# New lock rule and new due steps in the list scheduler of a recurrent-attention and gated-feed-forward kernel

## The chip, the cores and the metric

The kernel runs on one core of a Trainium2 chip. The metric is the time of one execution on the device in microseconds (us); less is better. The profile is of one execution.

## What is computed

There are 8 batches. Each has 8 heads of 512 tokens and 32 state vectors, all of width 64. In every head tokens attend to states and states attend to tokens:

```python
a     = softmax(scale * x @ state.T)      # 512 x 32
xread = a @ state                         # 512 x 64
a2    = softmax(scale * state @ x.T)      # 32 x 512
sread = a2 @ x                            # 32 x 64
attn  = concatenate([xread, sread])       # 544 rows
```

The heads are laid side by side (8 x 64 = 512 columns), which gives 4,352 rows: 8 batches of 512 token rows and 32 state rows. They go through a feed-forward block with 2,048 hidden columns:

```python
h = x @ w_in          # 512 -> 2048
g = h * cos(h)
y = g @ w_out         # 2048 -> 512
```

The result is float32. The two weight matrices arrive as float64, so the kernel fetches 64-bit words and converts them on the chip.

## The kernel before

**Tiles.** The work runs in the transposed sense: hidden columns on partitions, tokens along the free axis. For one batch a tile is 128 hidden columns by 512 tokens, so a batch has 16 tiles, and a pair of batches has 32. `hidden` (L488) makes a tile in a PSUM bank with two matmuls, because the kernel first multiplies the states into `w_in` (`products`, L312, with the copies out of PSUM at L462): the attention weights then meet that small product and `xread` is never formed. Then comes the gate, four instructions in turn: `gate` on ACT (L564, rounding to an integer), `gate2` on DVE (L567, the remainder), `gate3` on ACT (L570, the cosine as a shifted sine) and `gate4` on DVE (L584, the product with h, to `g_all`). A bank comes free with `gate4`; in the first pair tiles use two banks in turn.

**Product with w_out.** The first half of the first batch uses plain matmuls (`first_product`, `second_product`, L640). All later ones use a scheme with seven block products in place of eight: class `Product` (L772 matmuls), which needs sums and differences of the gated tiles (`sub`, L715, on POOL and DVE) and of the weight blocks (`sums_of`, L1325, and `inner_weight`, L689, on POOL). The weight blocks so made are sent to DRAM (`blocks_kept`, L677 and L692) and fetched back into a ring of four (L706). From the second pair on the hidden matmul has its own seven-product form (L543), for which POOL makes sums of the weights (`sw_sums`, L521). Tile 32 is the first of these.

**Weights.** Each 1 MB (or 0.5 MB) piece of the weights is fetched as 64-bit raw words (`fetch`, L210) and converted by five instructions (`convert`): two on ACT (L223, L226), two on DVE (L229, L232) and one on POOL (L237).

**Attention.** For each batch: scores (L312 to the banks `at0`, `at1`), row maxima (L325, L343), spreading of a value per row by a 32x32 transpose (L332), subtraction (L348), exponentials (L352, L361), sums (L325), the inverse (`inverse`, L373 and L374), normalising (`norm1`, L393). The late part turns the second softmax (L400, L405), reads (L417), scales (L427 or L436) and keeps (L441, L446) the new states.

**What sets the order.** From tile 32 on the order is written out: `plan`, `later_pair` and the tables by step. The first pair, tiles 0 to 31 with their attention, their weight conversions and weight sums, is ordered by a list scheduler that runs when the program is built. `first_pair_tasks` makes a list of tasks, each with an engine, an estimated cost, what it reads and writes, a due step, and a flag `shares` that says it uses the ports that DVE and POOL share. `link` turns data names into dependences and due steps into due times:

```python
t.due = 22.0 + PACE * t.due if t.due is not None else 1e9
for u in after[t]:
    t.due = min(t.due, u.due - t.cost - .1)
```

`first_pair` then repeats: for each engine it takes, of the tasks whose predecessors are done and that could start within `NEAR` (0.3) of the earliest, the one with the least due time plus a penalty for starting later; of the engines' candidates it issues the one that starts first. The order in which tasks are issued is the order of the instructions on each engine. Before the change the scheduler remembers one interval, the last POOL task's, and a DVE task with `shares` that would start inside it is moved to its end. POOL tasks are never moved.

Of the kernel before, what the change touches and what calls it, by code (L numbers as in the profile page):

```python
# [22 lines left out]
def kernel(  # L23
# [46 lines left out]
    TEMPS = 4  # L70
# [177 lines left out]
    class Attention:  # L248
# [207 lines left out]
        def products_kept(self, nt, bank=None, c0=0, c1=WC, copy=None,  # L456
                          js=(0, 1)):
            to = at if bank is None else side_banks
            if c0 == 0:
                sw_of[self.b, nt] = sw_all[:, nt % 2]  # L460
            for j in js:
                (copy or nc.scalar.copy)(sw_of[self.b, nt][:, j, c0:c1],  # L462
                                         to[j][:, c0:c1])
# [254 lines left out]
    class Product:  # L718
# [4 lines left out]
        def __init__(self, name, pr, row):  # L723
            self.name, self.pr, self.row = name, pr, (pr.n, row)
            self.n = len(products)
            self.b, self.c = acc[1 - self.n % 2], acc[self.n % 2]
            self.in_place = name in ("p3", "p7", "p4")
            self.frees = name in ("p3", "p6", "p7", "p4")
            products.append(self)
            self.first = len(stage_list)  # L730
            stage_list.extend((self, k) for k in range(len(ORDER)))
# [391 lines left out]
    def first_pair_tasks():  # L1123
# [49 lines left out]
        def attention(b, k):  # L1173
# [30 lines left out]
            m2 = k + 6 if b == 0 else k + 5  # L1204
            if b == 0:
                for j in range(2):
                    add("dve", .62, lambda j=j: a.sums1((j,)), f"z{z}{j}",
                        f"m1{j}", k + 5)
                add("dve", .46, a.inverse1, "m10 m11", "m10 m11", k + 5)
                for j in range(2):  # L1210
                    add("dve", .62, lambda j=j: a.spread1(slice(j, j + 1)),
                        f"m1{j}", f"xT{j}", k + 5)
                for j in range(2):
                    add("dve", .62, lambda j=j: a.norm1(slice(j, j + 1)),
                        f"z{z}{j} xT{j}", f"z{z}{j}", k + 5, True)
# [3 lines left out]
            if b == 0:  # L1219
# [4 lines left out]
                add("dve", .3, a.inverse2, "i20 i21", "i20 i21", m2 + 2)  # L1224
            else:
                add("act", 5.0, a.exps, "at0 at1 m20 m21",
                    f"z{z}0 z{z}1 xT2 xT3 i20 i21 m20 m21", m2)
                for j in range(2):
# [3 lines left out]
                    "m10 m11 i20 i21", k + 7)  # L1232
# [164 lines left out]
        def p5_tasks(k):  # L1397
# [3 lines left out]
            for i, (r, w) in enumerate(((lo, q1), (hi + " " + q1, q1),  # L1401
                                        (lo + " " + hi, q3)), 1):
                add("pool", 4 * pool(512), lambda i=i: pd.sums(i), r, w,
# [3 lines left out]
            for i in range(5):  # L1407
# [12 lines left out]
                elif i == 2:  # L1420
                    add("dve", .36, follow, "acc0 sums1", "sums2", at_)
                    add("pool", 4 * pool(512), lambda: pd.sums(4),
# [6 lines left out]
        def p3_sums(k):  # L1429
            pd = products_[1]  # L1430
            add("pool", 4 * pool(512), lambda: pd.sums(1),
# [17 lines left out]
        for step, what in (  # L1449
                (1, lambda: attention_late(0, 1)),  # L1450
                (3, lambda: products(0, 1, 3)),
                (3, lambda: add("pe", .4, lambda: states(1, side_banks[0]),
                                "held0", "sd00 sd01", 6)),
                (3, lambda: add("act", .53,
                                lambda: states_kept(1, side_banks[0]),
                                "sd00 sd01", "stT1", 6)),
                (5, lambda: attention(1, 5.0)),
                (7, lambda: products(0, 2, 7)),
                (11, lambda: products(0, 3, 11)),
                (13, lambda: products(1, 0, 15)),  # L1460
                (13, lambda: attention_late(1, 14)),
                (13, lambda: inner(0, a11, 5, temps[0], names(TEMPS), 15)),
                (15, lambda: sends(2, a22, 8, 17)),
                (15, lambda: sums_of(SQ, A21, A22, add_, 16, "pool")),
                (16, lambda: products(1, 1, 19)),
                (16, lambda: inner(3, matrix(SQ), SQ, temps[1], E, 15)),
                (17, lambda: sums_of(A22, SQ, A11, sub_, 18, "pool")),
                (17, lambda: attention(2, 18)),
                (18, lambda: sums_of(A21, A11, A21, sub_, 19, "dve")),
# [4 lines left out]
                (21, lambda: inner(4, matrix(A22), A22, temps[1], E, 21)),  # L1474
                (23, lambda: sums_of(SQ, A12, A22, sub_, 24, "dve")),
                (24, lambda: inner(6, matrix(SQ), SQ, temps[0], names(TEMPS),
                                   25)),
                (24, lambda: products(1, 3, 27)),
                (25, lambda: attention_late(2, 23.0)),
# [4 lines left out]
        for step, what in (  # L1484
                (26, lambda: outer(0, 2, 0, 0, 26, "dve")),
                (27, lambda: outer(0, 2, 0, 1, 27, "dve")),
                (28, lambda: tokens_of_next(30)),
                (28, lambda: products(2, 0, 28)),
                (28, lambda: p5_tasks(29.5)),
                (29, lambda: weight_columns(t32, 30)),  # L1490
                (29, lambda: add("dve", .7, lambda: halves(2, 0), "z00 z01",
                                 "E0", 30)),
                (29, lambda: add("dve", .7, lambda: halves(2, 1),
                                 "z00 z01 E0", "E1", 30)),
                (30, lambda: seven_tasks(t32, 30)),
# [4 lines left out]
        for step, t in enumerate(all_tiles[0:FIRST]):  # L1500
# [3 lines left out]
            if 4 <= step < 4 + NH:  # L1504
                first(step - 4, step + 1)
            for i in range(NH):
                if SECOND_AT[i] == step:
                    second(i, step + 2)
# [6 lines left out]
    CONV_DUE = (3, 4.5, 3.5, 6, 7.5, 7, 9, 9.5, 10.5, 11, 12, 14.5, 14, 15)  # L1515
    PACE, NEAR, SEND = 3.8, 0.3, 2.5

    def link(tasks):
# [20 lines left out]
        for t in reversed(tasks):  # L1539
            t.due = 22.0 + PACE * t.due if t.due is not None else 1e9  # L1540
            for u in after[t]:
                t.due = min(t.due, u.due - t.cost - .1)
# [11 lines left out]
    def first_pair():  # L1554
# [20 lines left out]
        pool_busy, cold = (0.0, 0.0), True  # L1575
        log = []
        while can:
            best = None
            for e in free:
# [4 lines left out]
                for t in mine:  # L1584
                    at_ = max(free[e], ready[t])
                    if t.shares and pool_busy[0] <= at_ < pool_busy[1]:
                        at_ = pool_busy[1]
                    starts[t] = at_
                soon = min(starts.values())
                t = min((t for t in mine if starts[t] <= soon + NEAR),  # L1590
                        key=lambda t: t.due + 1.0 * (starts[t] - soon))
                if best is None or starts[t] < best[0]:
                    best = starts[t], t
            at_, t = best
# [11 lines left out]
            if t.engine == "pool":  # L1606
                pool_busy = at_, end
# [139 lines left out]
```

## Time and profile before

| | |
|---|---|
| median of 3 runs | 739.78 us (738.67 to 739.96) |
| profiled execution | 740.65 us |
| its span, first to last instruction | 738.9 us |
| mean granted clock of TensorE | 0.993 |
| TensorE (PE) busy | 708.2 us, 96% |
| VectorE (DVE) busy | 506.8 us, 69% |
| ScalarE (ACT) busy | 347.3 us, 47% |
| GpSimd (POOL) busy | 542.5 us, 73% |
| first tile's matmul (L488) starts | 23.35 us |
| tile 31's last matmul (L488) ends, first pair over on TensorE | about 160.1 us |

The profiler gives one row for each instruction: its start, its length, its line in the kernel and, where its engine stood idle before it, what released it. A table of stretches gives the busy time of each engine between two moments. Rows on one engine may overlap by about 0.1 us, since the start of one instruction falls into the end of the one before. An instruction that waits inside the engine, for a port for example, shows as a longer row and not as idle time.

### The profile page before, as it was taken

What the parts mean: (1) busy time and instruction counts of PE and PEld (TensorE: products, weight loads), DVE (VectorE), ACT (ScalarE), POOL (GpSimd) and SP (SyncE); (2) the same over time, 40 slices, a digit from 0 to 9 for tenths busy, and PEclk for the clock granted to TensorE, in tenths of its full rate; (3) what the DMA queues carried; (4) which work ended last, traced back from release to release, by engine and by line L of the source; (5) the groups of instructions that cost most, each with busy time, mean ns of one, the idle gap of its engine ahead of it and who ended that gap; (6) DMA issues with size and microseconds to landing.
All of it is one profiled execution on the core that took longest, in us unless ns stands there. A gap on an engine that the chain in (4) does not pass through costs nothing.

```text
span 738.9 us, 10734 instructions
## 1 busy us (share of the span) xinstructions
PE 708.2 (96%) x3626; PEld 519.0 (70%) x3626; DVE 506.8 (69%) x703; ACT 347.3 (47%) x586; POOL 542.5 (73%) x524
## 2 busy tenths in 40 slices
PE   8898889999999999999999999999999999999997
PEld 3343343477778878777778788777688788888886
DVE  4989979957866668849756577768665467355550
ACT  5799675654463446343634464344634533211110
POOL 1557789375998997588998665879989665799600
PEclk9999999999999999999999999999999999999999
DMA  9966799536346964693238635762225466456662
GB/s 297 285 192 193 236 265 301 122 96 150 87 128 117 214 172 115 142 197 86 82 80 168 160 96 116 147 154 83 75 68 119 115 205 143 108 156 203 155 152 46
DMA packets 204021, 111.33 MB, mean 151 GB/s; under 512 B 149888, under 2 KB 166784, under 8 KB 203968
## 3 DMA queue, kind: packets, MB, share of 16 engines
q1 hardware_dynamic: 202880, 110.14, 57.4%
q8 instruction: 29, 0.48, 0.3%
q10 hardware_dynamic: 960, 0.39, 0.2%
q14 instruction: 24, 0.20, 0.1%
q0 software_dynamic: 128, 0.13, 0.1%
HBM read 87.03 MB, written 23.59 MB: 150 GB/s over the span
## 4 chain that ended last, share of the span: by engine, by line
PE 59%; POOL 21%; DVE 9%; issue 3%; DMA 3%; ACT 2%; SPq 1%; ACTq 0%; POOLq 0%; DVEq 0%
PE o L772 29%; POOL g_all L715 16%; PE h L543 13%; PE h L488 8%; POOL swS_all L521 3%; PE at L312 3%; PE at L877 2%; DMA held<-in_state_dram 2%; PE o L640 2%; POOL sw_all L521 2%; DVE g_all L715 1%; PE at L417 1%; DVE q_all L567 1%; DVE g_all L232 1%; DVE g_all L584 1%
## 5 line engine op out<-in xcount | busy, mean ns | idle before, releaser
L715 POOL TENSOR_TENSOR g_all<-g_all 128x512 f32<-128x512 f32 x252 | 332.5, 1349 | 61.8 <-DVE g_all L715 40.4
L772 PE MATMUL o<-g_all 128*128 128x256 f32 x1456 | 343.7, 381 | 2.4 <-POOL g_all L715 2.4
L772 PEld LDWEIGHTS o<-g_all 128*128 128x128 f32 x1456 | 273.7, 190 | 49.7 <-issue 5.7
L567 DVE TENSOR_TENSOR q_all<-q_all,h 128x1024 f32<-128x1024 int32 (+1 forms) x88 | 85.3, 971 | 40.7 <-ACT q_all L564 40.4
L564 ACT ACTIVATE q_all<-h 128x1024 int32<-128x1024 f32 (+1 forms) x88 | 73.1, 833 | 81.2 <-PE h L543 35.1
L584 DVE TENSOR_TENSOR g_all<-h,q_all 128x1024 f32<-128x1024 f32 (+1 forms) x88 | 85.7, 973 | 24.5 <-ACT q_all L570 23.6
L570 ACT ACTIVATE q_all<-q_all,halfpi 128x1024 f32<-128x1024 f32 (+1 forms) x88 | 84.2, 957 | 38.7 <-DVE q_all L567 38.5
L551 DVE TENSOR_TENSOR h<-h,sums_all 128x256 f32<-128x256 f32 x96 | 41.3, 430 | 77.5 <-PE h L543 60.2
L488 PE MATMUL h<-aT_all,sw_all 128*128 128x512 f32 x128 | 64.0, 628 | 13.0 <-DVE g_all L584 12.3
L543 PE MATMUL h<-aT_all,sw_all 128*128 128x256 f32 x192 | 59.6, 392 | 3.8 <-DVE g_all L584 3.4
L543 PE MATMUL h<-aS_all,swS_all 128*128 128x256 f32 x192 | 60.2, 395 | 2.6 <-ACT sums_all L529 1.8
L715 DVE TENSOR_TENSOR g_all<-g_all 128x1024 f32<-128x1024 f32 x42 | 62.0, 1490 | 0.1
L543 PE MATMUL h<-aS_all,sw_all 128*128 128x256 f32 x192 | 58.0, 384 | 0.1
L488 PEld LDWEIGHTS h<-aT_all,sw_all 128*128 128x128 f32 x128 | 23.2, 195 | 44.3 <-issue 21.5
L521 POOL TENSOR_TENSOR swS_all<-sw_all 128x128 f32<-128x128 f32 x48 | 22.5, 468 | 41.8 <-ACT sw_all L462 41.8
L543 PEld LDWEIGHTS h<-aS_all,swS_all 128*128 128x128 f32 x192 | 33.9, 189 | 27.0 <-issue 12.1
L780 ACT COPY o<-o 128x256 f32<-128x256 f32 x26 | 9.3, 357 | 85.1 <-PE o L772 85.1
L543 PEld LDWEIGHTS h<-aT_all,sw_all 128*128 128x128 f32 x192 | 34.5, 189 | 16.3 <-DVE g_all L584 12.2
L237 POOL TENSOR_TENSOR w_in<-w_in,aS_all 128x1024 int32<-128x1024 int32 (+1 forms) x10 | 22.3, 2241 | 29.9 <-DVE w_in L232 27.2
L787 ACT COPY o<-sums_all 128x256 f32<-128x256 f32 x26 | 9.8, 378 | 68.2 <-PE o L772 68.2
L543 PEld LDWEIGHTS h<-aS_all,sw_all 128*128 128x128 f32 x192 | 35.6, 190 | 8.2 <-DVE h L551 2.7
L607 DVE SCALAR_TENSOR_TENSOR held<-o,held 128x512 f32<-128x512 f32 x38 | 25.9, 681 | 13.7 <-PE o L772 13.1
(116 smaller groups left out, 931.6 us busy)
## 6 DMA issues: line engine op xcount, KB each, us to landing
g_all<-blocks_kept SPq DMA_DIRECT2D x206, 256.0 KB, 2.8
blocks_kept<-g_all SPq DMA_DIRECT2D x48, 256.0 KB, 3.9
g_all<-in_moe_w_out_dram SPq DMA_DIRECT2D x8, 1024.0 KB, 5.7
out_dram<-ot SPq DMA_DIRECT2D x128, 64.0 KB, 2.0
g_all<-in_moe_w_in_dram SPq DMA_DIRECT2D x6, 1024.0 KB, 7.1
x_b<-in_x_dram SPq DMA_DIRECT2D x24, 256.0 KB, 4.7
xT<-in_x_dram SPq DMA_DIRECT2D x80, 64.0 KB, 2.8
x_b<-in_x_dram SPq DMA_DIRECT2D x16, 128.0 KB, 4.3
```

The source lines that it names most:

```text
L237: nc.gpsimd.tensor_tensor(bits, bits, e, op=ALU.add)
L488: nc.tensor.matmul(out=t.hp, lhsT=t.lhs(i), rhs=t.rhs(i), start=(i == 0), stop=(i == t.kn - 1))
L521: nc.gpsimd.tensor_tensor(o, x1, x2, op=op)
L543: nc.tensor.matmul(out=out_, lhsT=w, rhs=r, start=start, stop=True, skip_group_check=True)
L551: nc.vector.tensor_tensor(o, h2[:, LO], sums_all[:, 0], op=ALU.add)
L564: nc.scalar.activation(t.q.bitcast(I32), t.hp, func=ACTF.Copy, bias=0.25)
L567: nc.vector.tensor_tensor(t.q, t.q.bitcast(I32), t.hp, op=ALU.subtract)
L570: nc.scalar.activation(t.q, t.q, func=ACTF.Sin, bias=halfpi, scale=-TWO_PI)
L584: nc.vector.tensor_tensor(g, t.hp, t.q, op=ALU.mult)
L607: nc.vector.scalar_tensor_tensor(out=out.t[:, ch], in0=bank, scalar=TWO_PI, in1=b.t[:, ch], op0=ALU.mult, op1=ALU.add)
L715: engine.tensor_tensor(o[:, i:i + n], x1[:, i:i + n], x2[:, i:i + n], op=ALU.subtract)
L772: nc.tensor.matmul(out=o, lhsT=ring[(self.first + k) % NB][:, i], rhs=g[:, i], start=(start and i == 0), stop=(i == QT - 1), skip_group_ch ...
```

## The change

The scheduler's model of the shared ports is replaced. There is now one time, `lock`, at which the ports come free. Every POOL task, and every DVE task with `shares`, starts no earlier than `lock`, and sets it to its own end. The penalty for starting later rises from 1.0 to 8.0 for each microsecond. Between engines that could start at the same time, the one whose task asked first goes first. Three kinds of DVE tasks get the flag: the inverses of the softmax sums and the differences of `halves`. The estimated cost of POOL's sums for the p5 and p3 products is halved (each makes two instructions of 512 elements a partition, not four). With this rule the due steps of nearly all tasks are set anew, `PACE` goes from 3.8 to 3.4, and the margin in `link` from 0.1 to 0.05. The test of when a batch's weight buffer is first written no longer asks for column 0, since the second half may now be copied first. No instruction of the computation changes.

```diff
-            if c0 == 0:
+            if (self.b, nt) not in sw_of:
                 sw_of[self.b, nt] = sw_all[:, nt % 2]
...
-            m2 = k + 6 if b == 0 else k + 5
+            m2 = k + 6 if b == 0 else k + 4
...
-                add("dve", .46, a.inverse1, "m10 m11", "m10 m11", k + 5)
+                add("dve", .46, a.inverse1, "m10 m11", "m10 m11", k + 5,
+                    True)
...
-                add("pool", 4 * pool(512), lambda i=i: pd.sums(i), r, w,
+                add("pool", 2 * pool(512), lambda i=i: pd.sums(i), r, w,
...
-                (1, lambda: attention_late(0, 1)),
-                (3, lambda: products(0, 1, 3)),
+                (1, lambda: attention_late(0, 0)),
+                (3, lambda: products(0, 1, 2.5)),
...
-                (5, lambda: attention(1, 5.0)),
-                (7, lambda: products(0, 2, 7)),
-                (11, lambda: products(0, 3, 11)),
-                (13, lambda: products(1, 0, 15)),
-                (13, lambda: attention_late(1, 14)),
+                (5, lambda: attention(1, 4)),
+                (7, lambda: products(0, 2, 4.5)),
+                (11, lambda: products(0, 3, 11.5)),
+                (13, lambda: products(1, 0, 16)),
+                (13, lambda: attention_late(1, 18)),
...
-                first(step - 4, step + 1)
+                first(step - 4, step - 1)
...
-                    second(i, step + 2)
+                    second(i, step)
...
-    CONV_DUE = (3, 4.5, 3.5, 6, 7.5, 7, 9, 9.5, 10.5, 11, 12, 14.5, 14, 15)
-    PACE, NEAR, SEND = 3.8, 0.3, 2.5
+    CONV_DUE = (3, 4.5, 3.5, 6, 6.7, 8.5, 9, 9.5, 12.0, 11, 11.3, 13.7, 12.5, 15.7)
+    PACE, NEAR, SEND = 3.4, 0.3, 2.5
...
-                t.due = min(t.due, u.due - t.cost - .1)
+                t.due = min(t.due, u.due - t.cost - 0.05)
...
-        pool_busy, cold = (0.0, 0.0), True
+        lock = 0.0
+        cold = True
...
-                    at_ = max(free[e], ready[t])
-                    if t.shares and pool_busy[0] <= at_ < pool_busy[1]:
-                        at_ = pool_busy[1]
-                    starts[t] = at_
+                    asked = max(free[e], ready[t])
+                    shares = t.shares or e == "pool"
+                    starts[t] = max(asked, lock) if shares else asked
                 soon = min(starts.values())
                 t = min((t for t in mine if starts[t] <= soon + NEAR),
-                        key=lambda t: t.due + 1.0 * (starts[t] - soon))
-                if best is None or starts[t] < best[0]:
-                    best = starts[t], t
-            at_, t = best
+                        key=lambda t: t.due + 8.0 * (starts[t] - soon))
+                asked = max(free[e], ready[t])
+                if best is None or (starts[t], asked) < best[0:2]:
+                    best = starts[t], asked, t
+            at_, _, t = best
...
-            if t.engine == "pool":
-                pool_busy = at_, end
+            if t.shares or t.engine == "pool":
+                lock = end
```

## The prediction

> **What bounds the kernel now.** I read the table of stretches first, then TensorE's waits, then the instructions in order of time, and last the order in which each kernel's instructions stand on their engines (no time is in that). The change touches only the first pair (tiles 0 to 31, until 160 us), so the question is what that part loses.
>
> ```profile
> 34.00:50.00 16.00, 15.07 (x77) 7.02 (x77) 12.01 (x20) 14.18 (x22) 9.55 (x5) 1.00 0.70 189
> 50.00:66.00 16.00, 16.00 (x66) 6.57 (x51) 15.22 (x21) 15.07 (x22) 12.16 (x7) 1.00 0.64 182
> 66.00:82.00 16.00, 11.67 (x60) 4.46 (x58) 15.73 (x20) 15.08 (x22) 11.11 (x6) 1.00 0.68 197
> 82.00:98.00 16.00, 11.30 (x61) 4.61 (x62) 15.77 (x16) 9.37 (x15) 12.67 (x7) 0.87 0.88 266
> 98.00:114.00 16.00, 15.58 (x60) 7.20 (x59) 12.30 (x14) 10.80 (x23) 15.84 (x10) 0.91 1.01 289
> 114.00:130.00 16.00, 14.84 (x67) 6.05 (x66) 15.93 (x22) 9.27 (x16) 15.84 (x12) 1.00 0.92 296
> 130.00:146.00 16.00, 15.66 (x68) 7.98 (x67) 14.52 (x20) 11.00 (x24) 6.61 (x5) 1.00 0.52 123
> ```
>
> The columns are PE, PEld, DVE, ACT and POOL busy, then TensorE's clock, DMA share and GB/s. Between 66 and 98 DVE is full (15.7 of 16) and PE is not (11.7, 11.3). That is the hole; from 98 on PE is nearly full, and from 250 to 700 it is 97 to 100% busy.
>
> ```profile
> PE h L488 <- DVE g_all L584: 12.3, 9, 3.5
> PE h L488 <- DVE aT_all L393: 0.7, 1, 0.7
> ```
>
> Of 14.4 us that PE idles in 20 to 162 us, 12.3 are nine waits of a tile's matmul (L488) for gate4 (L584) of the tile two before, which must give back the PSUM bank. So DVE's progress to L584 is the bound. What DVE loses is seen here:
>
> ```profile
> 83.19 3.40 DVE L232 SCALAR_TENSOR_TENSOR g_all<-g_all 128x1024 int32<-128x1024 int32 x1
> ...
> 83.17 2.34 POOL L237 TENSOR_TENSOR g_all<-g_all,aS_all 128x1024 int32<-128x1024 int32 x1
> ...
> 82.73 2.90 PE L488 MATMUL h<-aT_all,sw_all 128*128 128x512 f32 x4 [2.02 <-DVE g_all L584]
> ...
> 97.27 3.68 PE L488 MATMUL h<-aT_all,sw_all 128*128 128x512 f32 x4 [3.48 <-DVE g_all L584]
> ```
>
> L232 takes 1.22 us undisturbed; started with POOL's L237 it took 3.40, the 2.34 of POOL plus its own. Against the shortest row of each form, the stretched rows are: L232 +2.18 and +0.95; L229 +1.60, +0.46, +1.07, +1.07, +1.06; L373 +1.48; L393 +0.97; L1325 +0.48, +0.36. Sum 11.7 us in 50 to 103 us. L567 and L584, which read PSUM, stay at 0.68 throughout.
>
> **The change part by part.** No instruction of the first pair is added or removed except one 0.86 us warm-up matmul (11 become 12 after the opening two); everything else is order. After tile 31 the listed orders agree but for where one product stage stands among seven-product parts at the seam.
>
> *Opening.* ACT now puts the seventh conversion load (L223 to g_all), whose row waits for its transfer until 23.16, ahead of the copies of its weights (L462) out of PSUM, without which tile 0 cannot start. L223 1.05, L405 0.6, L462 twice 0.33: tile 0 can start at about 25.5, and with one read of 1.0 ahead of it at 25.9, not 23.35. Queued behind L223 are those copies and every gate; PE waits. But DVE does one L232 (1.13) after gate4 of tile 0 that it did before it, and gate4 waits only for its sine: ACT L564 at 27.7, L226, table load 1.28, L570 to 31.2, gate4 to 32.2, tile 2 at 32.6, not 34.21. Then the order turns on tile 3: L232, the inverse and four L427 (1.16) stand ahead of gate4 of tile 1, so tile 3 starts at 36.7 (was 36.05) and gate4 of tile 2 ends at 40.7 (was 40.63). Opening: 0, taken as a loss of 2.5 won back.
>
> *DVE from gate4 of tile 2 to gate4 of tile 14, the path to tile 16.* Counted start to start (L232, L715, L1325 1.13; L229, L567, L584 0.60; transposes and reductions 0.61), the order before has 42.4 us there, the new one 40.0: one weight sum (1.13), one L229 and one L567 (0.60 each) now stand later. It took 97.1 - 40.6 = 56.5 us, 14.1 more: 9.3 of the stretched rows above, 3.5 of idle (0.79, 1.54, 0.25, 0.54, 0.20, 0.19 in DVE's rows), 1.3 of small pieces. The new rule makes a ports task wait for the lock and, with weight 8 in place of 1, takes another task meanwhile; it also marks the inverses and the differences of `halves` as sharing, which L373 at 2.03 us says they are. Bounds: none of the 9.3 goes, or all.
>
> Row against rule: L232's 3.40 fits the Trainium skill, "SBUF — State Buffer", "Who interferes with whom": the pair is an exclusive lock and issue order, not the kind of operation, decides who blocks. That speaks against the change, since a list fixes order on one engine but not when POOL, freed by a semaphore, begins. By the rows avoided one by one the gain is 9.3; by the rule with drifting times it may be 0. I take half, 4.7, as the old scheduler had a lock test too and was still caught 11 times. Idle I put at 4.5, not 3.5: four times (tiles 7/8, 9/10, 10/11, 13/14) ACT now has the next tile's L564 ahead of this tile's sine. So 40.7 + 40.0 + 4.7 + 4.5 + 1.3 = 91.2 and tile 16 at 91.3, not 97.27: **6.0 us**.
>
> *PE from tile 16 to the end of tile 31.* One more first product (1.72) stands before tile 16, so 1.7 less is left, **+1.7**; it fits the hole, as PE idled there. Idle after tile 16 was 0.42 + 1.16 + 0.34 = 1.9; I allow 3.0, since DVE meets two L1325 and two L325 before gate4 of tile 22 and three L715 near tiles 24 to 26: **-1.1**.
>
> *Clock.* Tile 16 took 3.68 where 1.88 is usual, tile 13 2.90. By "TensorE: Matmul & The Clock Gate", "HAM oscillation — how this bites in real kernels", idle gaps over some 3.4 us slow the clock. The rows differ: the clock fell to 0.71 in 82 to 86 after gaps of 0.97 and 2.02 with PE busy 1.98 us of 78 to 82. By the rule the shorter gaps I expect cost nothing and tile 16's 1.80 comes back; by the rows it may stay. Half: **+0.9**.
>
> *POOL, SP.* POOL does one conversion and weight sums in another order; sends wait for the sums, nothing on PE waits for the sends in this stage. POOL idles 7.79 before L521 at 149.03 and again 4.79 and 5.00 at 165 to 177, so a backlog of several us is covered; without it, L521 (four of 0.46) is what seam parts of tile 32 would wait for. SP's opening five rows and its weight fetches keep their order; batch 2's x loads move by one send and batch 3's token loads behind the output stores, and their first reader (L294) is at 174, tens of us later. The scheduler's halved price of the p5 sums only alters places: 0.
>
> *After the seam.* The 580 us from tile 32 are the same queue, led by PE and by POOL in step; POOL's 5.00 wait at 176.75 ends with DVE's L715 of 175.49, itself in the fixed order. The block shifts as it is: 0.
>
> Sum 6.0 + 1.7 - 1.1 + 0.9 = 7.5 us. The profiled execution took 740.65 (span 738.9 and 1.75 around it), so 733.15; it stands 0.87 above the median 739.78, so the median should be 732.3. With none of the lock loss gone the sum is 2.8, with all of it 12.1: 737.0 to 727.7.
>
> **The rivals.**
>
> *The lock is the real bound and only moves.* Laid over each other, POOL's rows and DVE's sharing rows cover 74.4 of the 80 us from 50 to 130. If nothing of that work leaves the stretch, 5.6 us is all it can give, and stalls come back under other names: a gain of 2.8, 737.0. For it: POOL 15.84 of 16 twice. Against: the coverage holds waiting rows, and the sums can lag to 130 to 146, where POOL is busy 6.61 of 16.
>
> *Paired gates (slower).* At the four places named, tile n's bank comes free only after tile n+1's matmul, its conversion (0.5), sine (0.63) and gate4 (0.6) with latencies: about 2.5 us after PE ended tile n+1, of which PE has 1.0 to 1.7 of other work. I have counted about 1 us each. If a sharing instruction between them (L232 and two L393 stand at tiles 9 to 11) also meets POOL, each costs 1.2 more, and with a throttled restart of 1.8 each 4 us: 4 x 4 - 4 = 12 more than summed, so slower by 4.5, 744.3. It decides from about 2.9 us each on. For it: 2 us gaps throttled before. Against: DVE has the same number of such instructions as before.
>
> *POOL's backlog eats it at the seam.* If p5's first sums end past 148, not 134, tile 32's parts wait and the gain is swallowed: 0, 739.8. Against it the 7.79 us of POOL idle.
>
> *The change does nothing:* excluded, the order on every compute engine differs from about 20 us on.
>
> **How the numbers follow.** About 0.2%, 1.5 us, is what a measurement of this kernel can tell from no change. Summed forecast 0.62; lock only moves 0.18; paired gates 0.12; seam 0.08. Faster 0.62 + 0.18 = 0.80, same 0.08, slower 0.12. The range runs from all of the lock loss gone (728) to just short of no change (739), leaving out most of the slower case and of the seam case.
>
> **What would show it.** Right: last L488 of tile 31 ends near 152.6, not 160.07; tile 16 starts near 91; rows of L229, L232, L373 and L393 near their shortest; PE's wait for L584 falls from 12.3 to about 8; tile 0 starts near 25.9; the time from tile 32 to the end unchanged. Wrong: stretched DVE rows still add up to 10 us or more, L584 late at tiles 9 to 14 behind ACT L564, or L521 late at the seam.

## The result and the profile after

| | before | after |
|---|---|---|
| median of 5 runs each | 739.78 us (738.62 to 740.0) | 734.44 us (733.02 to 736.23) |
| profiled execution, its span | 740.65, 738.9 us | 736.23, 734.4 us |
| tile 16 starts | 97.27 us | 97.23 us |
| tile 31's last matmul ends (start of the instruction behind it) | 160.07 us | 155.54 us |

The changed kernel takes 0.993 of the time, 95% interval 0.991 to 0.9949: 5.3 us by the medians, 4.5 us between the two profiled spans. Predicted were 732.3 us and 7.5 us. The 4.5 us are all there when tile 31 ends; from there on the two traces run alike. The gain is not one of the clock: at a mean granted clock of 0.997 two runs of the changed kernel took 733.58 and 734.44 us, while eight runs of the kernel before, taken beside the experiments, took 738.37 to 740.84 us at 0.997 or 0.998.

The table of stretches of the changed kernel (PE, PEld, DVE, ACT, POOL busy, then TensorE's clock, DMA share, GB/s), in the same stretches as before:

```profile
34.00:50.00 16.00, 15.19 (x65) 7.03 (x64) 14.61 (x23) 15.62 (x24) 9.96 (x5) 1.00 0.67 180
50.00:66.00 16.00, 16.00 (x66) 6.62 (x65) 15.41 (x21) 14.03 (x22) 10.11 (x7) 1.00 0.60 197
66.00:82.00 16.00, 12.79 (x58) 4.76 (x56) 12.60 (x21) 12.72 (x17) 8.46 (x4) 0.89 0.60 193
82.00:98.00 16.00, 13.06 (x70) 6.01 (x71) 10.91 (x16) 14.36 (x27) 13.83 (x8) 1.00 0.74 226
98.00:114.00 16.00, 16.00 (x64) 7.51 (x63) 13.94 (x15) 9.39 (x16) 14.70 (x9) 1.00 0.87 239
114.00:130.00 16.00, 16.00 (x57) 6.65 (x55) 14.83 (x23) 11.61 (x20) 15.77 (x12) 1.00 1.00 318
130.00:146.00 16.00, 15.01 (x92) 6.84 (x92) 15.08 (x20) 10.87 (x25) 8.75 (x7) 1.00 0.76 175
```

Between 66 and 98 us DVE was full before; now it is busy 23.5 of 32 us, and PE still has a hole there (25.9 of 32). Neither engine is full: each waits for the other. The groups of DVE in 66 to 98 us of the changed kernel say what it waits for (busy, mean ns, then idle time ahead of the group and what ended it):

```profile
L584 DVE TENSOR_TENSOR g_all<-h,q_all 128x512 f32<-128x512 f32 x9 | 6.1, 690 | 4.1 <-ACT q_all L570 3.9
L232 DVE SCALAR_TENSOR_TENSOR g_all<-g_all 128x1024 int32<-128x1024 int32 x5 | 6.0, 1218 | 0.0
L567 DVE TENSOR_TENSOR q_all<-q_all,h 128x512 f32<-128x512 int32 x9 | 5.9, 675 | 4.0 <-ACT q_all L564 4.0
```

All five L232 of this group now take their undisturbed 1.22 us; before, five took 8.4 us in this stretch, 1.67 each. POOL's rows did not grow in exchange: it was busy 101.5 us of 18 to 160 before and 101.0 after. Instead DVE stands idle 8.1 us ahead of gate2 and gate4, for the rounding and the sine on ACT; before it was 0.4 us in that stretch. PE's waits in 20 to 162 us (total, times, longest):

```profile
PE h L488 <- DVE g_all L584: 5.6, 6, 1.9
PE at L417 <- ACT xT L405: 4.3, 3, 2.8
PE at L441 <- DVE sr L427: 0.6, 1, 0.6
```

The wait for gate4 fell from 12.3 to 5.6 us. And the instructions of PE in order of time, at the two places that matter below:

```profile
69.57 2.70 PE L488 MATMUL h<-aT_all,sw_all 128*128 128x512 f32 x4 [1.92 <-DVE g_all L584]
72.06 2.91 PE L640 MATMUL o<-g_all 128*128 128x512 f32 x4
...
93.69 1.98 PE L488 MATMUL h<-aT_all,sw_all 128*128 128x512 f32 x4 [1.07 <-DVE g_all L584]
95.51 1.88 PE L640 MATMUL o<-g_all 128*128 128x512 f32 x4
97.23 1.88 PE L488 MATMUL h<-aT_all,sw_all 128*128 128x512 f32 x4
```

Tile 9 waits 1.92 us and then it and the product behind it take 2.70 and 2.91 us instead of 1.88: the granted clock fell, to a mean of 0.59 in 70 to 74 us. Tile 16 starts as late as before, though it no longer waits; what is gained comes after it.

**How much DVE is stretched.** One number is used below for every kernel: over the rows of L229, L232, L373, L393, L507, L715 and the weight sums (L1325, here L1328) on DVE between 18 and 160 us, the busy time less the count times the undisturbed length (L232, L715 and sums 1.22 us for 1024 elements, L229 and L393 0.69 and 0.68, L373 0.17, half forms by their own shortest row). It is 20.8 us before and 13.7 us after. It is not by itself a measure of speed: in the table below e5_rule has the lowest value and is the slowest kernel, and e10_half has 17.2 and starts tile 16 first.

### The profile page after: what moved, and what is told of

It reads as the page before. It is cut to its first block, busy times and chain, and to the rows that moved or that the text cites. A ratio compares the mean times of both kernels' runs of the same rounds, so it can differ in the third digit from the quotient of the medians.

```text
span 734.4 us, 10738 instructions
## 1 busy us (share of the span) xinstructions
PE 707.4 (96%) x3628; PEld 518.9 (71%) x3628; DVE 499.6 (68%) x703; ACT 346.3 (47%) x586; POOL 541.2 (74%) x524
## 4 chain that ended last, share of the span: by engine, by line
PE 62%; POOL 21%; DVE 6%; ACT 5%; issue 3%; DMA 2%; SPq 1%; POOLq 0%; DVEq 0%; ACTq 0%
PE o L773 29%; POOL g_all L715 16%; PE h L543 13%; PE h L488 9%; POOL swS_all L521 3%; PE at L312 3%; PE o L640 2%; PE at L878 2%; DMA g_all<-in_moe_w_out_dram 2%; DVE g_all L715 2%; POOL sw_all L521 2%; PE at L417 2%; DVE g_all L584 1%; PE o L878 1%; DVE q_all L567 1%
## 5 line engine op out<-in xcount | busy, mean ns | idle before, releaser
L715 POOL TENSOR_TENSOR g_all<-g_all 128x512 f32<-128x512 f32 x252 | 333.5, 1354 | 59.5 <-DVE g_all L715 43.2
L543 PE MATMUL h<-aT_all,sw_all 128*128 128x256 f32 x192 | 59.6, 392 | 3.8 <-DVE g_all L584 3.4
L543 PE MATMUL h<-aS_all,swS_all 128*128 128x256 f32 x192 | 60.2, 395 | 2.6 <-ACT sums_all L529 1.8
L715 DVE TENSOR_TENSOR g_all<-g_all 128x1024 f32<-128x1024 f32 x42 | 60.9, 1465 | 0.1
L543 PE MATMUL h<-aS_all,sw_all 128*128 128x256 f32 x192 | 58.0, 384 | 0.2
L543 PEld LDWEIGHTS h<-aS_all,swS_all 128*128 128x128 f32 x192 | 33.9, 189 | 27.0 <-issue 12.1
L543 PEld LDWEIGHTS h<-aT_all,sw_all 128*128 128x128 f32 x192 | 34.5, 189 | 16.3 <-DVE g_all L584 12.1
L237 POOL TENSOR_TENSOR w_in<-w_in,aS_all 128x1024 int32<-128x1024 int32 (+1 forms) x10 | 21.4, 2153 | 29.9 <-DVE w_in L232 22.7
L543 PEld LDWEIGHTS h<-aS_all,sw_all 128*128 128x128 f32 x192 | 35.6, 190 | 8.3 <-DVE h L551 2.8
L607 DVE SCALAR_TENSOR_TENSOR held<-o,held 128x512 f32<-128x512 f32 x38 | 25.8, 680 | 13.7 <-PE o L773 13.1
```

The lines of the kernel that those rows point to most:

```text
L543: nc.tensor.matmul(out=out_, lhsT=w, rhs=r, start=start, stop=True, skip_group_check=True)
L607: nc.vector.scalar_tensor_tensor(out=out.t[:, ch], in0=bank, scalar=TWO_PI, in1=b.t[:, ch], op0=ALU.mult, op1=ALU.add)
L715: engine.tensor_tensor(o[:, i:i + n], x1[:, i:i + n], x2[:, i:i + n], op=ALU.subtract)
```

## The experiments

The variants of the changed kernel collect what the scheduler lists and move entries of that list before they are issued (`move` behind, `put` directly behind another entry), all dependences kept. Times are medians with lowest and highest; the ratio is to the kernel before, run on the same chip. Tile times are those of the profiled execution.

| kernel | median us | ratio, 95% interval | tile 9 | tile 16 | tile 31 ends | DVE stretched |
|---|---|---|---|---|---|---|
| before | 739.4 to 740.6 | 1 | 62.04 | 97.27 | 160.07 | 20.8 |
| after | 734.44 (733.02 to 736.23) | 0.993 [0.991, 0.9949] | 69.57 | 97.23 | 155.54 | 13.7 |
| e5_rule | 749.08 (743.89 to 753.07) | 1.0116 [1.0078, 1.0154] | 64.70 | 98.70 | 160.06 | 11.9 |
| e6_dues | 743.52 (742.74 to 746.05) | 1.0058 [1.0044, 1.0072] | 72.55 | 100.2 | 162.3 | 20.8 |
| e11_seam | 740.70 (739.25 to 741.96) | 1.0019 [1.0009, 1.0029] | 63.43 | 99.01 | 159.08 | 14.2 |
| e1_open | 735.33 (732.42 to 739.32) | 0.9943 [0.9921, 0.9966] | 67.28 | 96.63 | 155.6 | |
| e2_warm | 735.86 (732.25 to 736.78) | 0.9932 [0.9912, 0.9951] | 67.71 | 97.08 | 156.0 | |
| e3_gates | 736.16 (735.27 to 739.2) | 0.9954 [0.9937, 0.997] | 69.75 | 99.82 | 158.5 | |
| e4_both | 734.36 (733.91 to 735.4) | 0.9922 [0.9909, 0.9935] | 67.78 | 95.77 | 154.5 | 16.5 |
| e7_fill | 738.26 (736.86 to 738.75) | 0.9979 [0.9969, 0.9988] | 70.07 | 98.71 | 157.5 | |
| e8_best | 736.65 (736.37 to 737.46) | 0.9961 [0.9949, 0.9973] | 66.37 | 97.16 | 155.8 | 14.8 |
| e9_nofill | 735.92 (733.64 to 736.53) | 0.9953 [0.994, 0.9965] | 66.21 | 96.61 | 155.3 | 15.8 |
| e10_half | 734.11 (733.68 to 734.5) | 0.9934 [0.9921, 0.9948] | 66.15 | 94.19 | 152.95 | 17.2 |
| e12_early | 735.55 (735.37 to 737.81) | 0.9931 [0.9916, 0.9946] | 68.62 | 97.35 | 156.9 | |

**Which half of the change carries it: the rule or the due steps?**

e5_rule, the kernel before with the new rule:

```diff
-                    if t.shares and pool_busy[0] <= at_ < pool_busy[1]:
-                        at_ = pool_busy[1]
+                    starts[t] = max(asked, lock) if shares else asked
...
-                        key=lambda t: t.due + 1.0 * (starts[t] - soon))
+                        key=lambda t: t.due + 8.0 * (starts[t] - soon))
```

> The kernel before with the new rule of the shared ports alone (one release time, weight 8, the flags and the halved Pool costs); the due steps stay the old ones. Theory 1 (the rule carries the gain, by the DVE rows that a Pool operation no longer stretches): the stretched DVE rows between 18 and 160 us sum to about 14 us as in the changed kernel, not 21; tile 31 ends at 155 to 157 us instead of 160.1, and the time is 734.5 to 737. Theory 2 (the due steps carry it, by the order of conversions that they set, and the rule alone does little or harm): stretched rows may fall, but tile 31 ends at 159 or later and the time is 739 or more.

e6_dues, the changed kernel with the lock, the weight of 8 and the rule for ties turned back, and everything else kept:

```diff
-                    starts[t] = max(asked, lock) if shares else asked
+                    if t.shares and pool_busy[0] <= at_ < pool_busy[1]:
+                        at_ = pool_busy[1]
...
-                        key=lambda t: t.due + 8.0 * (starts[t] - soon))
+                        key=lambda t: t.due + 1.0 * (starts[t] - soon))
...
```

> The changed kernel with the old rule of the ports and the old weight of 1; the new due steps, flags and costs stay. Theory 1 (the rule carries the gain): stretched DVE rows return to about 20 us, tile 31 ends at 159 to 161 us, 738.5 to 741. Theory 2 (the due steps carry it): tile 31 ends at 155 to 157 us, 734 to 736.5, with stretched rows still near 20 us.

Neither theory was right: each half alone is slower than before, by 1.2% and 0.6%, and only both together are faster. With the due steps in place the rule is worth 1.3%, or 9 us (743.52 against 734.44). Its effect on DVE is confirmed: it takes the stretched rows from 20.8 to 11.9 us by itself, and the due steps alone leave them at 20.8. The same group of DVE, in 18 to 160 us, first of e6_dues, then of e5_rule:

```profile
L232 DVE SCALAR_TENSOR_TENSOR g_all<-g_all 128x1024 int32<-128x1024 int32 x8 | 13.2, 1655 | 0.2
```

```profile
L232 DVE SCALAR_TENSOR_TENSOR g_all<-g_all 128x1024 int32<-128x1024 int32 x8 | 9.7, 1222 | 0.1
```

How much of the 9 us is the shorter rows and how much the order that the new weight also changes was not separated. e6_dues loses its time ahead of tile 16 (2.9 us later than before): PE waits 2.22 us for POOL's conversion L237 and 2.07 us for gate4 there, and tile 9 and the product behind it then take 3.78 and 2.50 us.

In e5_rule tile 31 ends at 160.06 us, as before, and then the kernel loses 8.6 us more. The same instruction of the seam, the late product L312 into `at`, starts at 167.50 us before, at 162.98 after and at 176.06 in e5_rule. PE of e5_rule in order of time:

```profile
163.51 0.59 PE L543 MATMUL h<-aT_all,sw_all 128*128 128x256 f32 x2
163.94 0.59 PE L543 MATMUL h<-aS_all,swS_all 128*128 128x256 f32 x2
165.39 0.70 PE L543 MATMUL h<-aS_all,swS_all 128*128 128x256 f32 x2 [0.85 <-ACT sums_all L529]
165.93 0.59 PE L543 MATMUL h<-aT_all,sw_all 128*128 128x256 f32 x2
168.31 1.22 PE L543 MATMUL h<-aS_all,sw_all 128*128 128x256 f32 x2 [1.79 <-DVE h L551]
169.33 1.06 PE L543 MATMUL h<-aT_all,swS_all 128*128 128x256 f32 x2
```

The new rule listed the parts of the first seven-product tile one behind the other, after tile 31, where before and after have them spread between tiles and products. So each part waits for the sums of the last, and the clock falls too (0.79 in 162 to 178 us; from 168.31 on a row takes 1.06 to 1.22 where 0.59 to 0.70 is usual). The waits in these rows and the next are 3.2 us, the longer rows about 3, and four pairs of L543 more than before stand behind tile 31, 1.7 us. The six runs of e5_rule took from 743.89 us at a mean clock of 0.998 to 753.07 us at 0.984, so about half of the loss goes with the clock, and the rest is there without it.

e11_seam tests that: e5_rule with the new pace and, of the new due steps, only those from step 24 on.

```diff
-                (24, lambda: products(1, 3, 27)),
-                (25, lambda: attention_late(2, 23.0)),
+                (24, lambda: products(1, 3, 31)),
+                (25, lambda: attention_late(2, 25)),
...
-                (30, lambda: seven_tasks(t32, 30)),
+                (30, lambda: seven_tasks(t32, 29.5)),
...
-    PACE, NEAR, SEND = 3.8, 0.3, 2.5
+    PACE, NEAR, SEND = 3.4, 0.3, 2.5
```

> e5_rule (the kernel before with the new rule alone) with the new pace and those new due steps that stand at step 24 and later: the last products, the late part of the third attention, the sums of the second pair, and the first seven-product tile. Theory 1 (the rule alone lost its 9 us where that tile begins: its parts came behind tile 31, with waits and a clock of 0.79 at 162 to 178 us, and the late due steps put them between tiles 30 and 31 again): the waits of L543 between 163 and 173 us are gone and the time is 738 to 741, and what is left to the changed kernel (4 to 6 us) belongs to the early due steps. Theory 2 (the loss comes with the rule from the order of the early first products and gates): still 745 or more.

Theory 1 held: 1.0116 became 1.0019, the L312 of the seam is at 166.51 us, and no L543 waits there. So of the change's parts, the rule clears DVE, the late due steps together with the new pace repair the seam that the rule spoils, and the early due steps, with those of the conversions and the smaller margin, bring the rest: from 1.0019 to 0.993, some 6.6 us. Pace and late due steps were not tried apart. In e11_seam the cleared DVE is of no use, since PE then waits elsewhere, 8.3 us for gate4 and 4.4 for copies of weights out of PSUM (L462).

**Why the opening gave no lead.**

In the trace after, the opening is as predicted up to tile 0, but then slow. ACT, then PE, in order of time:

```profile
23.25 1.15 ACT L223 ACTIVATE g_all<-g_all 128x1024 f32<-128x1024 f32 x1 [2.23 <-DMA g_all<-in_moe_w_out_dram]
```

```profile
24.92 1.09 PE L417 MATMUL at<-x_b,xT 128*64 128x128 f32 x16 [2.78 <-ACT xT L405]
25.95 5.40 PE L488 MATMUL h<-aT_all,sw_all 128*128 128x512 f32 x8
```

Tiles 0 and 1 together take 5.40 us, where before they took 3.67. e1_open moves the conversion out of the way, e2_warm leaves it and puts three warm-up matmuls into the wait.

```diff
+        move(("convert", 6, "1"), ("turn_kept", 0, 1))
```

> The order of the changed kernel (734.4 us), one task moved: ACT's first conversion step of the seventh weight piece (L223 to g_all, whose transfer lands at about 23.2 us) goes behind the four copies that tile 0 and the first reads need. Theory: that step at the head of ACT's queue made TensorE wait 2.8 us, which delayed tile 0 from 23.35 to 25.95 and let its clock fall, so that tiles 0 and 1 took 5.4 us and not 3.7. Then tile 0 starts near 23.3, tiles 0 and 1 take 3.7, tile 2 starts 2 to 4 us before 34.7, and the time falls by 2 to 4 us, to 730.5 to 732.5. Rival: from tile 4 on ACT (15.6 of 16 us busy in 34 to 50) and DVE set the pace, so the head start is lost by tile 9 and the time stays at 734.4 within 0.7.

```diff
+        listed.insert(at_of(("reads", 0, 0)),
+                      (None, lambda: warm(3, acc[0]), None))
```

> The changed kernel with three more warm-up matmuls (2.6 us) on TensorE just before the first reads, in the 2.8 us for which it waits for ACT there. ACT's order stays. Theory: the clock fell because of that wait, so tiles 0 and 1 take 3.7 us instead of 5.4 while tile 0 still starts near 25.9; tile 2 starts up to 1.7 us earlier and the time falls by 1 to 1.7 us, to about 733. Rival: tile 2 waits for gate4 of tile 0 (ACT's table load and sine behind it) in any case and later engines set the pace: 734.4 within 0.7.

Both held the clock at the place: tiles 0 and 1 take 3.70 us in each. PE of e2_warm:

```profile
25.52 3.70 PE L488 MATMUL h<-aT_all,sw_all 128*128 128x512 f32 x8
```

Tile 2 then starts at 32.59 us in e2_warm and 32.02 in e1_open, not 34.71. (In e1_open tile 0 starts only 1.0 us earlier and PE still waits 2.19 us; L405 waited for DVE's norm1, until 23.29 us, instead of L223.) Yet tile 16 is at 97.08 and 96.63 us, and the ratios are those of the changed kernel within their intervals. Of a lead of 2.7 us in e1_open, 0.6 is left at tile 16. Tile 9 and its product are slow in both kernels, and 2.3 us of the lead are still there when tile 15 starts, 91.40 against 93.69 us. It goes here:

```profile
91.40 3.48 PE L488 MATMUL h<-aT_all,sw_all 128*128 128x512 f32 x4 [1.06 <-DVE g_all L584]
94.67 2.13 PE L640 MATMUL o<-g_all 128*128 128x512 f32 x4
```

In the changed kernel the same two took 1.98 and 1.88 us: 1.7 us of the lead are a fall of the clock. e2_warm loses 1.7 of its last 1.85 us at the same place.

**Are the paired gates the brake?**

e3_gates takes the gates of tiles 7/8, 9/10, 10/11 and 13/14 apart: on ACT gate of the second goes behind gate3 of the first, and on DVE gate2 of the second behind gate4 of the first. e4_both does this and e1_open's move.

```diff
+        for n in (7, 9, 10, 13):
+            move(("gate", n + 1), ("gate3", n))
+            move(("gate2", n + 1), ("gate4", n))
...
```

> The order of the changed kernel, with the paired gates of tiles 7/8, 9/10, 10/11 and 13/14 taken apart: gate of the later tile goes behind the sine of the earlier one on ACT, and gate2, gate3 and gate4 of the later one behind gate4 of the earlier one. Nothing else moves. Theory: the pairs made tiles 9, 11, 12 and 15 wait for a bank by 1.9, 1.0, 1.0 and 1.1 us, and the first of these waits also let TensorE's clock fall (1.9 us more at tile 9 and the product behind it). Then PE's wait for L584 falls from 5.6 to about 2 and the time falls by 2 to 5 us, to 729.5 to 732.5. Rival: the waits come from DVE's and ACT's whole load before tile 16, so they only change places: 734.4 within 0.7, or later by up to 1 us since gate4 of the later tile of each pair comes later.

> The opening as in e1_open and the gates as in e3_gates, together. If the two causes are apart the gains add: 4 to 8 us below 734.4, and tile 16 starts near 91, where the prediction had it. If the stretch to tile 16 is bound by DVE's and ACT's load, the sum is no better than the better of the two.

e3_gates gained nothing: 0.9954 against 0.993, the intervals overlap, and PE's wait for gate4 was 6.9 us. Its one run at a clock of 1.000 took 736.18 us, where that of the changed kernel took 733.02. e4_both is the lowest ratio of the study, 0.9922, but within the interval of the changed kernel; its clock was 0.998 or 1.000 in all five runs, and the fastest took 733.91 us, so its lead may be no more than the clock. So the pairs are not shown to cost anything by themselves.

**Does the clock take the leads?**

e7_fill puts zero-adding matmuls into the waits of e1_open (they add zeros to the accumulator of the products):

```diff
+        def fill(n):
+            for _ in range(n):
+                nc.tensor.matmul(out=acc[0], lhsT=zeros[:, 0:P], rhs=zeros,
+                                 start=False, stop=True,
+                                 skip_group_check=True)
+        listed.insert(at_of(("hidden", 9)), (None, lambda: fill(4), None))
```

and in the same way two each ahead of tile 11, tile 12, the late `reads` and tile 15.

> The kernel in which one conversion of the opening stands behind the second copy of the turned weights (e1_open), with zero-adding matmuls of 0.43 us put into TensorE's waits: four before tile 9, two each before tile 11, tile 12, the late product of the second attention and tile 15. They add zeros to the accumulator, so nothing is left out. Theory 1 (the leads before tile 16 are lost because TensorE's clock falls after waits of 1 to 2 us, and tiles then take 3.2 to 3.7 us): no tile L488 over 2.0 us between 60 and 100 us, granted clock 1.00 there, tile 16 starts at 94.5 to 95.5 us instead of 96.6, and the time is 732 to 734 with a smaller spread. Theory 2 (tile 16 is held by DVE's and ACT's chain of gates, the slow tiles only fill what would be a wait): tile 16 at 96.5 us again, the waits for L584 longer by what the tiles are shorter, 735 to 736.

e8_best does so on e4_both, with tiles 0 and 1 ahead of the first `reads`:

```diff
+        for j in range(2):
+            move(("turn_kept", 0, 0), ("sw", 0, 0, j))
+        move(("reads", 0, 0), ("hidden", 1))
```

> Everything that the runs so far point to, in one kernel: the changed order with the opening conversion moved, tiles 0 and 1 put ahead of the first product of the attention on TensorE and its copy behind those of the weights on ACT, the four pairs of gates taken apart (e4_both), and zero-adding matmuls in TensorE's waits before tiles 9, 11, 12, 13 and 15 (2, 4, 1, 3, 3). Theory 1 (clock and opening): tile 0 at 23.4 us, tile 2 at 31 to 32 us, tile 16 at 93.5 to 94.5 us, tile 31 ends at 150.5 to 152.5 us (e4_both: 154.5), time 731 to 733. Theory 2 (a later wait takes it: the chain of gates before tile 16, or the sums of the seven-product tiles): tile 16 not before 95.5 us, or its lead lost again by tile 31; 734 to 735.5.

Half of theory 1 came true in both: no slow tile between 60 and 100 us, clock 1.00, and runs close together (spread 1.9 us where e1_open has 6.9). But each was slower than the kernel it was made from (738.26 against e1_open's 735.33, 736.65 against e4_both's 734.36, and against 735.92 of e9_nofill, which is e8_best without the filler). The expectations sized a zero-adding matmul at 0.43 us; in the traces each makes two rows of 0.43 us, so e7_fill added 24 rows, 10.3 us, and e8_best 26, 11.2 us. PE was busy 31.8 and 32 of 32 us in 66 to 98: the filler was longer than the waits. The next two runs are e8_best with none and with five (ten rows, 4.3 us in truth):

> e8_best without its zero-adding matmuls. In e8_best TensorE had no wait between 66 and 98 us and no slow tile, but the added matmuls (13 of 0.43 us, 5.6 us) were longer than the waits that they filled. Theory 1 (they cost more than the clock's fall): tile 16 starts at 92 to 95.5 us instead of 97.2, tile 31 ends at 149 to 152.5 us instead of 156, the time is 731 to 734. Theory 2 (each lead ahead of tile 16 goes to a slow clock without them): one or two tiles of 3 us or more between 60 and 96 us, tile 16 at 96 to 97.5 us, 734 to 736, and the runs spread over 3 us or more.

> e8_best with 5 zero-adding matmuls (one before tile 9, two before 11, one each before 13 and 15; 2.1 us) instead of 13. Theory 1 (short pieces are enough to hold the clock, and now fit into the waits): no slow tile, tile 16 at 92.5 to 94.5 us, 731 to 733.5, spread under 1.5 us. Theory 2 (what is added comes on top, waits or not): tile 16 at 95.5 us or later, 734 to 736.

This pair is the test of the clock. Until tile 9 the two traces are equal (66.21 and 66.15 us). PE of e9_nofill:

```profile
74.71 3.65 PE L488 MATMUL h<-aT_all,sw_all 128*128 128x512 f32 x4 [2.06 <-DVE g_all L584]
...
91.38 3.25 PE L488 MATMUL h<-aT_all,sw_all 128*128 128x512 f32 x4 [1.98 <-DVE g_all L584]
94.42 2.35 PE L640 MATMUL o<-g_all 128*128 128x512 f32 x4
```

PE of e10_half at the same places, the zero-adding rows being L1652:

```profile
72.52 1.98 PE L1652 MATMUL o<-g_all 128*128 128x512 f32 x4
74.65 1.98 PE L488 MATMUL h<-aT_all,sw_all 128*128 128x512 f32 x4
...
89.05 1.12 PE L1652 MATMUL o<-g_all 128*128 128x512 f32 x2
90.65 1.98 PE L488 MATMUL h<-aT_all,sw_all 128*128 128x512 f32 x4 [0.47 <-DVE g_all L584]
```

Tile 11 starts at the same moment, so the filler cost nothing there, and what follows runs at full clock: tile 16 at 94.19 instead of 96.61 us, the span 732.1 instead of 734.1, the median 734.11 instead of 735.92. All five runs of e10_half had a mean clock of 0.999 or 1.000 and lie within 0.8 us; e9_nofill had 0.995 in four (735.39 to 736.53 us) and 1.000 in one, and that one took 733.64 us, like e10_half: nothing but the clock is seen to come from the filler. In e1_open the same shows across eight runs: 732.42 us at 0.999, 739.32 at 0.991. So the clock falls are shown to cost some 2 us per execution in e9_nofill and to make most of the spread there.

The clock is not all that holds these kernels. The changed kernel's own run at 1.000 took 733.02 us; no variant beats that by more than 0.8 us (732.25 and 732.42).

**Is it then the conversions ahead of tile 11?** e12_early is e10_half with some gates moved. It puts the gates of tiles 9 and 10 among three conversions that stood ahead of them, with one zero-adding matmul each ahead of tiles 9, 12, 13 and 15 (3.4 us):

```diff
+        for label, behind in (
+                (("gate", 9), ("hidden", 9)),
+                (("gate2", 9), ("convert", 14, "c")),
+                (("gate3", 9), ("convert", 15, "2")),
+                (("gate4", 9), ("convert", 15, "b")),
...
+            put(label, behind)
```

> e10_half with the gates of tiles 9 and 10 put among the three conversions that stand ahead of them on ACT and DVE, and the zero-adding matmuls moved with it: one each before tiles 9, 12, 13 and 15 (1.7 us). In e10_half gate4 of tile 9 ended at 74.5 us behind those conversions and held tile 11 until 74.65 us. Theory 1 (the order of DVE and ACT ahead of tile 11 is what holds TensorE once its clock is held): gate4 of tile 9 ends near 71 us, tile 11 starts at 72.5 to 73 us, tile 16 at 92 to 93 us instead of 94.2, tile 31 ends at 150.5 to 152 us instead of 153, time 732 to 733.3. Theory 2 (the conversions are only put off, and come back ahead of tiles 12 to 15, whose waits grow by what tile 11 gained): tile 16 at 94 us or later, 733.7 to 735.

Theory 2. From tile 9 to tile 11 e12_early needs 6.36 us, e10_half 8.50: the 2.1 us are gained. From tile 11 to tile 16 it needs 22.37 us against 19.54: they are given back. PE of e12_early:

```profile
78.40 1.09 PE L312 MATMUL h<-w_in,st_all 64*32 64x512 f32 x16 [1.43 <-ACT sw_all L462]
...
84.22 1.98 PE L488 MATMUL h<-aT_all,sw_all 128*128 128x512 f32 x4 [1.10 <-DVE g_all L584]
```

The copies of weights behind the same conversions on ACT are now late, then the gates of tile 11. Its profiled execution also lost about 2 us ahead of tile 9, to a wait for x of a batch and a clock of 0.89 in 34 to 50 us; it was the slowest of the five (737.81 us, the others 735.37 to 735.95). By the ratio, 0.9931, it equals the changed kernel and e10_half.

## Why the prediction was right, and which terms were not

The direction held, and so did the range (734.44 against 732.3 us) and the place: all of the gain is there when tile 31 ends, nothing comes after. The mechanism of the rule held too. But the sum was 7.5 us, of which 6.0 were to stand at tile 16 and 1.5 after it, and in the profiled execution it was 0.0 and 4.5. That the total still fell near the forecast is in part luck: the terms ahead of tile 16 cancelled, and those after it came larger than forecast.

- **Opening, 0.** The L223 ahead of the copies, the start of tile 0 (25.95, predicted 25.9) and its cause were right. gate4 of tile 2 ended at 42.64, not 40.7 us: tiles 0 and 1 ran 1.73 us longer behind the 2.78 us wait. With the clock held, e2_warm has tile 2 at 32.59, the predicted 32.6. The step failed by a clock fall, which was counted only for tile 16.
- **Lock loss, half of 9.3 left.** Better than taken: between gate4 of tile 2 and of tile 14 three rows are still stretched, L229 by 0.98, 1.83 and 0.74, 3.6 us where 4.7 was taken. (The 9.3 was itself a little low: L373 takes 0.18 us undisturbed in the trace after, not the 0.55 that it was measured against.) The doubt that the prediction drew from "SBUF — State Buffer", "Who interferes with whom" (issue order decides who blocks, to which it added that times drift), weighed too much: most avoided rows stayed avoided. e5_rule and e6_dues show that the rule does this and the due steps do not.
- **DVE idle, 4.5.** It was 6.8, in eight waits of up to 1.97 us. With these, 42.64 + 40.0 + 3.6 + 6.8 + 1.3 = 94.3, and gate4 of tile 14 ended at 94.24 us: the sum's form was right and this term too small. When DVE's time stopped being scarce, the chain of a gate over ACT and DVE, with PE behind it, became the bound; the idle time that the sum took from the trace of before belonged to a full DVE.
- **Tile 16 right behind gate4 of tile 14.** This was the larger miss: it started 3.0 us later. gate4 of tiles 13 and 14 come as a pair on DVE:

```profile
92.94 1.30 DVE L584 TENSOR_TENSOR g_all<-h,q_all 128x512 f32<-128x512 f32 x2 [0.19 <-ACT q_all L570]
```

So tile 15 itself waited for the first of them until 93.69, and tile 15 and the product that was to "fit the hole" (1.82 and 1.72 us from start to start) stood ahead of tile 16. The product did not lie beside a wait.

- **After tile 16, +1.7 - 1.1 + 0.9.** The product gave its 1.7. The idle time was 1.0 (0.35, 0.24, 0.40), not 3.0: +0.9. Tile 16's slow 1.80 came back whole, not half. Together 4.4 of the 4.5 us by which the spans differ.

Term by term the account closes. Up to tile 16 the opening lost 2.0 us, the DVE work that now stands later gave 2.4, the stretched rows gave 5.7, idle time took 3.3 and the later start of tile 16 took 2.9: -0.1. The clock falls ahead of tile 16 lie inside these terms and are not one more: 1.73 us at tiles 0 and 1 in the opening, and 1.85 us at tile 9 and its product, ahead of DVE's longest idle time.

Of the rivals, *the lock only moves* is refuted in its own form, since the stretched rows fell, POOL's rows did not grow and DVE idles some 8 of 32 us; what it said of stalls that come back under other names is true. Its ceiling was mis-read: laid over each other again, POOL's rows and DVE's sharing rows cover 77.7 of the 80 us before (76.7 after), not 74.4, so it allowed 2.3 us and not 5.6. *Paired gates* has its sign in the idle time, but taking them apart (e3_gates) did not give the time back. *POOL's backlog at the seam* did not happen after; in e5_rule the seam did cost 8.6 us, by another cause, the order of the parts of tile 32.

By the rule in "TensorE: Matmul & The Clock Gate", "HAM oscillation — how this bites in real kernels" (no idle gaps over some 3.4 us), the waits here would cost nothing. The rows contradict that for this kernel: behind waits of 1.06 to 2.06 us the clock fell to means of 0.59 to 0.74 over stretches of 4 us. The next section of the same page, "A second HAM failure mode: psum-queue depth-cycling", describes frequent short idles between groups of matmuls that go round PSUM banks, there in bf16, and is nearer to the pattern here.

Open stays what decides whether a given wait lets the clock fall (a 2.06 us wait ahead of tile 11 did so in e9_nofill, not in e4_both), and what bounds the first 98 us at about this time with the clock held: e12_early shows only that the conversions are not free to move. Open stays too which part of the rule, the lock or the weight of 8, does the work.

## What to carry to other kernels

A better model of one contended resource may pay only with the due steps that were set for it: here each half alone was slower than neither. When the engine that was full is cleared, work out the chain that comes next (here a tile's gate across ACT, DVE and PE) with its own latencies, and do not carry the idle time of the full engine over. Where TensorE works in short groups with waits of 1 to 2 us, count a possible slow group behind each, look at each run's clock before comparing medians, and try a short filler that ends ahead of the release: it is free only if it is shorter than the wait.

## What the runs showed of the hardware

- In several runs the clock of TensorE fell behind waits of about 1 to 2 us between groups of 2 to 4 us: tiles of 1.88 us took 2.70 to 3.65. Filler rows of 1 to 2 us inside such waits kept it at 1.00 through 66 to 98 us (e10_half). A wait does not always do it: e4_both had waits of up to 2.06 us there without filler, and 1.00.
- The same program on the same chip spread over 6.9 us (e1_open), in step with a mean clock of 0.991 to 0.999.
- A port wait can cost a tiny DVE instruction nearly as much as a large one. L373 on 34 elements a partition took 2.03 us before, beside POOL's L237, and 0.18 us after, with POOL idle: 1.85 us more, where L232 on 1024 elements lost 2.18. The rows, two of before and one of after:

```profile
70.84 2.03 DVE L373 TENSOR_SCALAR i_all<-i_all 128x34 f32<-128x34 f32 x1
70.47 2.37 POOL L237 TENSOR_TENSOR g_all<-g_all,aS_all 128x1024 int32<-128x1024 int32 x1 [1.23 <-DVE g_all L232]
...
71.78 0.18 DVE L373 TENSOR_SCALAR i_all<-i_all 128x34 f32<-128x34 f32 x1
```
